# Two unused tiles that move the operands of the one-pass products to multiples of 256 bytes

## The chip, the cores and the metric

The kernel runs on one core of a Trainium2 chip. The metric is the device time of one execution in microseconds. Lower is better.

## The reference, cut to what matters

Two layers, each a linear attention block and an MLP, over 2048 rows of 448 columns in float32:

```python
x = A_x
x = x + _A_ref(_layernorm(x, axis=-1), A_wqkv, A_wo)
x = x + _B_ref(_layernorm(x, axis=-1), B_w1, B_b1, B_w2, B_b2)
x = x + _A_ref(_layernorm(x, axis=-1), A_wqkv, A_wo)
x = x + _B_ref(_layernorm(x, axis=-1), B_w1, B_b1, B_w2, B_b2)
```

`_A_ref` projects x to q, k and v with 16 heads of 28, maps q and k by `phi(t) = where(t > 0, t + 1, exp(t)) + 1e-6`, forms `kv = pk^T v` and `z = sum(pk)` for each head, divides `pq kv` by `pq z + 1e-6` and multiplies by `wo`. `_B_ref` is `gelu(x w1 + b1) w2 + b2` with 1792 hidden columns and the tanh form of gelu.

## The kernel before, in words

**Tiles.** The 2048 rows are 16 tiles of 128, and in the MLP four blocks of four tiles. Every product is float32 in accuracy, but most of them run as one-pass products: both operands are split into a high part of type fp32r and a remainder of type fp32r (`hi`, `lo`), and three products (hi hi, hi lo, lo hi) go into one PSUM bank. A product here is one weight load of the stationary operand (128 columns, PEld in the profile) and one matmul with the moving operand (448 or 512 columns). `pe.matmul(out, stationary, moving, ...)` is the order of the arguments; in the profile's names (`y<-w2h,gh`) the moving operand stands first. Some small products take plain float32 operands and two passes: kvp (L641), mp (L651), zp (L621).

**Stages of a layer.** Phase 1 (`phase1`, L553) walks over the 16 tiles: layer norm, transposes, the projections psk and psq (`proj`, L299, 11 products of 448 columns each) and G (`stage_g`, L475, 11 products). The transition (`ORDER`, L494) turns G into the matrices M for the attention output, and makes the output op of the four tiles of block 0 (`o_mm`, L727, 12 products each). Then comes the MLP: for each block and each of 14 slices i of the hidden columns, `mlp1` (L795) makes hp with 11 products of 512 columns, ACT and DVE make its gelu and split it into gh and gl, and `mlp2` (L814) makes 12 products y of 448 columns, three for each of the block's four tiles. The product of slice i + 1 is issued ahead of y of slice i. Into the steps of a block `behind` (L876) puts the attention output of the next block by a plan written out by hand, in which op comes from `oc_mm` (L736) with 11 products, four times a block.

The order of all instructions is fixed by the program (`tc.manual_schedule()`), and each engine runs its own in that order.

**Where operands lie.** On-chip memory is handed out by pool, in the order `consts`, `wts`, `work`, each pool behind the one before. In a pool, tiles lie in the order in which their tag is first asked for, one tile for each buffer of the tag, and each begins at the next multiple of 32 bytes behind the one before. So an unused tile shifts all that is first asked for after it. All offsets are bytes within a partition. Before the change, in the program as built:

| pool | tiles, in order | offset mod 256 |
|---|---|---|
| consts | ones, ident, mhalf, tiny, zc, mask, b1s, b2b | ones and ident 128 |
| consts | none, za and zb, dc | none 224, za 0 |
| wts | w1h, w1l, w1x, w2h, w2l | 64 |
| work | H (x), S (staging, squares, Mh and half of Ml) | 64 |
| work | bst, bmv, bve, brs (three buffers each, each in 32 bytes) | from 64 on |
| work | tail, W and V pieces (wk, wq, pq), XH, XL, A (xnh, gh), B (xnl, gl), e, E (kh, qh), F (kl, ql, half of Ml), xn | 192 |
| work | dn, rd | 192 and 64 |

Within a tile, the pieces that products read begin at multiples of 512 bytes (128 columns) or 1792 bytes (448 columns), which are multiples of 256, so an operand has the offset mod 256 of its tile. The moving operand of hp is four runs of 128 columns, 2048 bytes apart (`moving`, L224); all other moving operands are one run.

Of the kernel before, what the change touches and what calls it, by code (L numbers as in the profile page):

```python
# [9 lines left out]
F32 = mybir.dt.float32  # L10
# [12 lines left out]
def linear_attn_mlp_kernel(  # L23
# [26 lines left out]
    consts = ctx.enter_context(tc.tile_pool(name="consts", bufs=1))  # L50
    wts = ctx.enter_context(tc.tile_pool(name="wts", bufs=1))
    work = ctx.enter_context(tc.tile_pool(name="work", bufs=2))
# [121 lines left out]
                       compare_op=OP.is_ge, fill=0.0)  # L174
    b1s = consts.tile([128, NF], F32, name="b1s")
    b2b = consts.tile([128, D], F32, name="b2b")

    w1h = wts.tile([128, 3, F], F32R, name="w1h")
    w1l = wts.tile([128, 3, F], F32R, name="w1l")
# [11 lines left out]
    def ln_bn(xs):  # L191
        st = work.tile([128, 6], F32, name="bst", tag="bst", bufs=3)
        dve.bn_stats(st, xs)
        return st

    def ln_stats(xs, st=None):
        st = ln_bn(xs) if st is None else st
        mv = work.tile([128, 2], F32, name="bmv", tag="bmv", bufs=3)
        dve.bn_aggr(mv, st)
        ve = work.tile([128, 1], F32, name="bve", tag="bve", bufs=3)  # L200
        dve.tensor_scalar(ve, mv[:, 1:2], 1e-5, None, op0=OP.add)  # L201
        rs = work.tile([128, 1], F32, name="brs", tag="brs", bufs=3)
        pool.tensor_tensor(rs, ve, mhalf, op=OP.pow)  # L203
        return xs, mv, rs
# [172 lines left out]
    def stage_a(l, t):  # L377
        sts[l, t] = ln_stats(xt.pop((l, t)))

    def stage_n(l, t):  # L380

        xs, mv, rs = sts.pop((l, t))
        dve.tensor_scalar(xs, xs, mv[:, 0:1], rs, op0=OP.subtract, op1=OP.mult)
        xns[l, t] = xs
        if t < TURNED[l]:
            d = tails[l, t] = work.tile([128, 128], F32, name="tail", tag="tail", bufs=2)
            act.copy(d.rearrange("p (u n) -> p u n", u=2), xs[:, None, TL:].to_broadcast([128, 2, 64]))
# [521 lines left out]


    stage_a(0, 0)
    bn = ln_bn(xt[0, 1])
    stage_n(0, 0)
    split_hi("k", 0, st_k)
# [4 lines left out]
    for l in range(LAYERS):  # L919
# [27 lines left out]
        for tok in ORDER.split():  # L947
            name, j = tok.rstrip("0123456789"), int("0" + tok.lstrip("abcdefghijklmnopqrstuvwxyzQTG"))
# [69 lines left out]
```

## Time and profile before

| what | value |
|---|---|
| time, median of 3 runs | 885.9 us (885.64 to 886.61) |
| the profiled execution | 884.81 us |
| its span, first to last instruction | 883.1 us |
| PE busy | 877.8 us, 4182 matmuls |
| DVE, ACT, POOL busy | 489.9, 343.5, 220.8 us |

The page of the profile lists busy times by engine, the chain of work that ended last, and groups of instructions by line. The timeline lists single instructions with their start and duration in us. In the answer by windows each row is a stretch of time, its length, and for each engine its busy time with the number of instructions in it, then the granted clock of PE, the DMA share and GB/s. PE's durations overlap: a matmul's start and the next one's start are nearer to one another than its duration is long.

### The profile page before, as it was taken

The page shows a single profiled execution, that of the slowest core. Times are in us where ns is not written, and L with a number is a line of the kernel's source. Part 1 is how long each engine was busy: PE and PEld are TensorE (multiplying, and loading weights), DVE is VectorE, ACT ScalarE, POOL GpSimd, SP SyncE. Part 2 cuts the span into 40 slices and gives each one's busy share as a digit, 9 for nine tenths or more (in the row PEclk, how much of TensorE's full clock was granted, in tenths as well). Part 3 has the DMA queues.
Part 4 walks back from the last instruction along what each step waited for, and adds up shares of the span by engine and source line. Part 5 has one row for each costly group of instructions (what it writes and reads, how often), then busy time and mean ns, then how long its engine had stood idle before and what let it go on. Part 6 is the DMA issues. An engine that isn't in the chain of part 4 may idle for free.

```text
span 883.1 us, 11676 instructions
## 1 busy us (share of the span) xinstructions
PE 877.8 (99%) x4182; PEld 773.0 (88%) x4182; DVE 489.9 (55%) x953; ACT 343.5 (39%) x603; POOL 220.8 (25%) x250
## 2 busy tenths in 40 slices
PE   9999999999999999999999999999999999999998
PEld 8999888888888888888899998988888888888887
DVE  6878585658455443226477876864664373433112
ACT  5676635334323322333356565332232233233221
POOL 5566532335013102012222344210320140130000
PEclk9999999999999999999999999999999999999999
DMA  5475637633313402051146543352332423111001
GB/s 157 135 231 165 199 88 211 180 99 118 131 59 104 154 0 96 1 178 48 48 133 192 164 127 105 113 171 79 116 106 84 136 72 108 49 48 42 1 1 42
DMA packets 63482, 94.76 MB, mean 107 GB/s; under 512 B 8896, under 2 KB 58560, under 8 KB 63424
## 3 DMA queue, kind: packets, MB, share of 16 engines
q1 hardware_dynamic: 63424, 94.01, 34.0%
q8 instruction: 33, 0.54, 0.3%
q14 instruction: 25, 0.20, 0.1%
HBM read 56.17 MB, written 34.60 MB: 103 GB/s over the span
## 4 chain that ended last, share of the span: by engine, by line
PE 96%; DMA 1%; DVE 1%; ACT 1%; issue 0%; SPq 0%; POOL 0%; DVEq 0%; ACTq 0%; POOLq 0%
PE y L820 10%; PE y L821 10%; PE y L819 10%; PE hp L801 9%; PE hp L803 9%; PE hp L802 9%; PE hp L805 3%; PE hp L804 3%; PE psq L308 2%; PE psq L307 2%; PE psq L306 2%; PE psk L307 2%; PE G L482 2%; PE G L483 2%; PE psk L308 2%; PE G L481 2%
## 5 line engine op out<-in xcount | busy, mean ns | idle before, releaser
L811 DVE TENSOR_TENSOR gl<-g,gh 128x512 fp32r<-128x512 f32 x112 | 83.1, 742 | 306.3 <-ACT gh L810 306.3
L807 ACT ACTIVATE g<-hp,b1s 128x512 f32<-128x512 f32 x112 | 77.2, 689 | 412.5 <-PE hp L805 409.2
L820 PE MATMUL y<-w2l,gh 128*128 128x448 f32 x448 | 164.6, 367 | 0.0
L821 PE MATMUL y<-w2h,gl 128*128 128x448 f32 x448 | 164.0, 366 | 0.0
L819 PE MATMUL y<-w2h,gh 128*128 128x448 f32 x448 | 162.9, 364 | 0.0
L801 PE MATMUL hp<-XH,w1h 128*128 128x512 f32 x336 | 132.8, 395 | 0.0
L803 PE MATMUL hp<-XL,w1h 128*128 128x512 f32 x336 | 132.4, 394 | 0.0
L802 PE MATMUL hp<-XH,w1l 128*128 128x512 f32 x336 | 132.1, 393 | 0.0
L203 POOL TENSOR_TENSOR brs<-bve,mhalf 128x1 f32<-128x1 f32 x64 | 39.5, 617 | 286.5 <-DVE bve L201 283.4
L820 PEld LDWEIGHTS y<-w2l,gh 128*128 128x128 f32 x448 | 84.1, 188 | 10.1
L819 PEld LDWEIGHTS y<-w2h,gh 128*128 128x128 f32 x448 | 84.1, 188 | 9.8
L821 PEld LDWEIGHTS y<-w2h,gl 128*128 128x128 f32 x448 | 84.2, 188 | 6.1
L803 PEld LDWEIGHTS hp<-XL,w1h 128*128 128x128 f32 x336 | 63.1, 188 | 15.1 <-issue 0.5
L802 PEld LDWEIGHTS hp<-XH,w1l 128*128 128x128 f32 x336 | 63.6, 189 | 11.7
L801 PEld LDWEIGHTS hp<-XH,w1h 128*128 128x128 f32 x336 | 63.0, 188 | 11.8
L810 ACT CAST gh<-g 128x512 fp32r<-128x512 f32 x112 | 69.6, 622 | 3.6
L694 POOL TENSOR_TENSOR pz<-pq,zb 128x448 f32<-128x448 f32 x32 | 36.8, 1154 | 87.2 <-DVE dn L700 76.1
L416 POOL TENSOR_TENSOR xnl<-x,xnh 128x384 fp32r<-128x384 f32 x32 | 35.1, 1095 | 71.7 <-ACT xnh L415 39.6
L296 DVE TENSOR_TENSOR XL<-sp,XH 128x512 fp32r<-128x512 f32 x50 | 44.4, 894 | 4.2 <-ACT XH L295 4.2
L805 PE MATMUL hp<-XL,w1x 128*128 128x512 f32 x112 | 44.4, 397 | 0.0
L804 PE MATMUL hp<-XH,w1x 128*128 128x512 f32 x112 | 44.0, 393 | 0.0
L763 POOL TENSOR_TENSOR x<-x,b2b 128x448 f32<-128x448 f32 x32 | 42.0, 1332 | 0.0
(146 smaller groups left out, 1565.0 us busy)
## 6 DMA issues: line engine op xcount, KB each, us to landing
x<-in_A_x_dram SPq DMA_DIRECT2D x32, 224.0 KB, 3.8
pq_d<-eq SPq DMA_DIRECT2D x32, 224.0 KB, 2.9
pq<-pq_d SPq DMA_DIRECT2D x32, 224.0 KB, 3.2
sq_m<-sq SPq DMA_DIRECT2D x14, 512.0 KB, 2.8
sp<-sq_m SPq DMA_DIRECT2D x56, 128.0 KB, 3.0
x<-x_d SPq DMA_DIRECT2D x32, 224.0 KB, 3.4
sq_a<-sq SPq DMA_DIRECT2D x12, 512.0 KB, 2.9
sp<-sq_a SPq DMA_DIRECT2D x48, 128.0 KB, 3.1
```

Source lines behind the costliest of these rows:

```text
L296: eng.tensor_tensor(lo.rearrange("p (c i n) -> p c i n", c=4, n=32), x, f(h), op=OP.subtract)
L801: pe.matmul(o, w1h[:, c, s], x.moving(x.hi, c), start=(c == 0), stop=False)
L802: pe.matmul(o, w1l[:, c, s], x.moving(x.hi, c), start=False, stop=False)
L803: pe.matmul(o, w1h[:, c, s], x.moving(x.lo, c), start=False, stop=False)
L804: pe.matmul(o, w1x[:, s], x.moving(x.hi, 3), start=False, stop=False)
L805: pe.matmul(o, w1x[:, s], x.moving(x.lo, 3), start=False, stop=True)
L807: act.activation(g, hp, AF.Gelu_apprx_tanh, bias=b1s[:, i:i + 1])
L810: act.copy(gh, g)
L811: dve.tensor_sub(gl, g, f(gh))
L819: pe.matmul(acc[j], gh[:, s], w2h[:, i], start=first, stop=False)
L820: pe.matmul(acc[j], gh[:, s], w2l[:, i], start=False, stop=False)
L821: pe.matmul(acc[j], gl[:, s], w2h[:, i], start=False, stop=last)
```

## The change

One tile of 192 bytes is asked for in `consts` behind b2b, one of 128 bytes in `work` behind the small tiles of the first layer norm. Nothing reads or writes either. Of the tiles in the table, ones, ident and those up to b2b stay where they are; all others move.

```diff
     b1s = consts.tile([128, NF], F32, name="b1s")
     b2b = consts.tile([128, D], F32, name="b2b")
+    consts.tile([128, 48], F32, name="space")
 
     w1h = wts.tile([128, 3, F], F32R, name="w1h")
...
     stage_a(0, 0)
+    work.tile([128, 32], F32, name="space", tag="space", bufs=1)
     bn = ln_bn(xt[0, 1])
     stage_n(0, 0)
```

## The prediction

> **What bounds the kernel now.** I read the page first (span, busy shares, granted clock, the chain that ended last), then the groups by line, then the timeline of the tensor engine, stage by stage.
>
> ```profile
> span 883.1 us, 11676 instructions
> PE 877.8 (99%) x4182; PEld 773.0 (88%) x4182; DVE 489.9 (55%) x953; ACT 343.5 (39%) x603; POOL 220.8 (25%) x250
> PEclk9999999999999999999999999999999999999999
> PE 96%; DMA 1%; DVE 1%; ACT 1%; issue 0%; SPq 0%; POOL 0%; DVEq 0%; ACTq 0%; POOLq 0%
> ```
>
> The chain of work that ended last lies on PE for 96% of the span, and the clock was granted in full throughout. So whatever the change does, it does by the rate of PE's products. The engines behind them wait for PE:
>
> ```profile
> L811 DVE TENSOR_TENSOR gl<-g,gh 128x512 fp32r<-128x512 f32 x112 | 83.1, 742 | 306.3 <-ACT gh L810 306.3
> L807 ACT ACTIVATE g<-hp,b1s 128x512 f32<-128x512 f32 x112 | 77.2, 689 | 412.5 <-PE hp L805 409.2
> L820 PE MATMUL y<-w2l,gh 128*128 128x448 f32 x448 | 164.6, 367 | 0.0
> L821 PE MATMUL y<-w2h,gl 128*128 128x448 f32 x448 | 164.0, 366 | 0.0
> L819 PE MATMUL y<-w2h,gh 128*128 128x448 f32 x448 | 162.9, 364 | 0.0
> L801 PE MATMUL hp<-XH,w1h 128*128 128x512 f32 x336 | 132.8, 395 | 0.0
> L803 PE MATMUL hp<-XL,w1h 128*128 128x512 f32 x336 | 132.4, 394 | 0.0
> L802 PE MATMUL hp<-XH,w1l 128*128 128x512 f32 x336 | 132.1, 393 | 0.0
> L805 PE MATMUL hp<-XL,w1x 128*128 128x512 f32 x112 | 44.4, 397 | 0.0
> L804 PE MATMUL hp<-XH,w1x 128*128 128x512 f32 x112 | 44.0, 393 | 0.0
> ```
>
> ACT waits 409.2 us for hp, DVE 306.3 us behind ACT. There are 3 x 448 = 1344 y products and 3 x 336 + 2 x 112 = 1232 hp products. The mean durations here (364 to 397 ns) overlap and are no rates. The rate is the pitch, the distance from one start to the next, and that needs the timeline and counts by window. A window's PEld count is the number of weight loads that began in it, one for each product:
>
> ```profile
> 65.51:81.11 15.60, 15.60 (x79) 14.46 (x77) 14.19 (x29) 10.23 (x20) 8.94 (x12) 1.00 0.58 184
> 277.08:282.08 5.00, 5.00 (x25) 4.32 (x23) 4.20 (x9) 1.83 (x3) 2.65 (x3) 1.00 0.00 0
> 874.22:878.91 4.69, 4.69 (x25) 4.32 (x23) 2.06 (x4) 1.31 (x2) 0.00 (x0) 1.00 0.00 0
> ```
>
> - Attention stage (psk, psq and G): 15.60 us / 77 = 202.6 ns a product of 448 columns.
> - The last y products, which follow one another without hp: 4.69 / 23 = 203.9 ns, also 448 columns.
> - One step of the MLP (12 y, 11 hp): 5.00 us. With y at 203.9 ns, hp takes (5000 - 2447) / 11 = 232.1 ns.
>
> G (L481 to L485) and y (L819 to L821) have the same shape and the same rhythm, three products to a PSUM bank, and their stationary operands even lie in the same buffers (xnh and gh in A, xnl and gl in B). Only the moving operand differs: kh and kl begin 192 bytes past a multiple of 256, w2h and w2l 64 bytes past one. Higher address bits don't matter: from one i to the next, w2 moves on by 1792 bytes and A and B change buffers, and the step stays at 5.00 us. Nor does the stage itself matter: where 11 op products (moving wq at 192, stationary qh and ql at 192) join an MLP step, these two starts lie 12 + 11 + 11 = 34 products apart:
>
> ```profile
> 171.50 0.36 PE L819 MATMUL y<-w2h,gh 128*128 128x448 f32 x1
> ...
> 178.73 0.36 PE L819 MATMUL y<-w2h,gh 128*128 128x448 f32 x1
> ```
>
> That is 7.23 us, 2.23 more than the 23, so 202.7 ns for each op: the attention rate, in the MLP stage. I read from it that a product pays for how the low address bits of its moving operand stand to those of the stationary operand that is loaded beside it. An equal offset mod 256 (192 and 192) gives 202.6 ns, and a distance of 128 (y: 64 and 192) gives 203.9.
>
> **The change part by part.** Neither tile is ever used, so no instruction, wait or DMA is added, taken away or reordered; every queue issues what it did. Only addresses move. In the program as built before, the weights w1 and w2 and the tiles H and S begin at 64 mod 256, and the small tiles follow; the work tiles W, V, XH, XL, A, B, e, E, F and xn begin at 192 mod 256. The first space adds 192 bytes ahead of the weights: 64 + 192 = 256. The second adds 128 behind the four kinds of small tile: 192 + 192 + 128 = 512. So every one-pass operand comes to 0 mod 256, and hp (moving 192, stationary 64) and y (moving 64, stationary 192) go from a distance of 128 to a distance of 0.
>
> - **y**: 1344 x (203.9 - 202.6) = 1.7 us less.
> - **hp**: no row shows a 512-column product at distance 0. From one side, it gains what y gains, 1.3 ns. From the other, its whole surplus falls to that of the attention products. For the surplus I need a floor, and take it from the two-pass products:
>
> ```profile
> 109.25 3.31 PE L641 MATMUL kvp<-gt,stg 128*112 128x112 f32 x32
> 115.50 3.17 PE L651 MATMUL mp<-wot,kvm 112*112 112x448 f32 x8
> L641 PE MATMUL kvp<-gt,stg 128*112 128x112 f32 x64 | 6.6, 262 | 0.0
> L651 PE MATMUL mp<-wot,kvm 112*112 112x448 f32 x16 | 6.3, 539 | 0.0
> ```
>
> Less the last one's own duration, 32 kvp start at (3310 - 262) / 31 = 98.3 ns and 8 mp at (3170 - 539) / 7 = 375.9 ns: 0.826 ns a column and 5.8 ns fixed. Half of that a column, and the same fixed part, would make a one-pass product of 448 columns 190.8 ns and one of 512 columns 217.3 (an estimate). The surplus over this floor is then 11.8 ns in attention, 13.1 for y and 14.8 for hp, and hp would gain 3.0 ns. hp could also gain nothing, if its surplus comes from reading four runs of 128 columns. Between 1.3 and 3.0 I take 2.0, nearer the y row: 1232 x 2.0 = 2.5 us less.
> - **op of block 0 (L732 to L734)**: Mh and two of four Ml lie at 64 in S, against A and B at 192: 80 of 96 products, 1.3 ns each, 0.1 us less.
> - **psk, psq, G, op by chunks**: 32 x 33 + 24 x 11 = 1320 products. Distance 0 before and after, so nothing, unless the offset itself matters; that is unknown. At most they gain their 11.8 ns, 15.6 us.
> - **The other engines**: their operands move too. Were each of their instructions a little slower or faster, the waits above (409.2 and 306.3 us) hide it. It costs only where PE waits for them, and the chain gives DVE and ACT 1% each.
> - **DMA**: same sizes and order, 1% of the chain; nothing.
>
> Sum: 1.7 + 2.5 + 0.1 = 4.3 us. The profiled execution took 884.8 us (span 883.1 and 1.7 around it), 1.1 under the median of 885.9. The sum is a difference, so I take it off the median: 881.6 us. With hp at nothing or at 3.0 ns, this case's own range is 880 to 884.1. PE stays the bound: a step of 4.96 us still holds only 4.20 us of DVE and 1.83 of ACT.
>
> **A rule against it.** The row: 203.9 and 202.6 ns at one shape, 13.1 and 11.8 over the floor. The Trainium skill ("TensorE: Matmul & The Clock Gate", Step-by-step: what each phase is for) says that PE reads moving and stationary operands through two independent ports, so that loading the next weights takes no read bandwidth from the running matmul. By that rule no distance between the two could matter, and the sum would be 0 instead of 4.3 us; the rows for y and G disagree, though they can't say whether the port or something behind it is shared.
>
> **Rivals.**
>
> *Nothing changes (885.9 us).* The difference between G and y has another cause than offsets, such as the steps of w2 itself. For it: 1.3 ns is 0.6% of a pitch. Against it: equal shapes, equal rhythm, equal stationary buffers, and op at 202.7 in the same stage. The Trainium skill ("SBUF — State Buffer", Specifications (TRN2)) gives lines of 16 bytes; by that line size every operand is aligned already and 256 brings nothing. No row here shows a line's size.
>
> *The alignment itself pays (about 874 us).* A 448-column row of 1792 bytes that begins at 64 or 192 touches 8 pieces of 256 bytes, an aligned one 7; a weight load of 512 bytes touches 3, then 2. For hp, the four runs of 512 bytes touch 12, then 8. If the surplus over the floor goes with the pieces, it falls from 11 to 9 for 448 columns and from 15 to 10 for 512: 13.1 x 0.18 x 1344 = 3.2 us, 11.8 x 0.18 x 1416 = 3.0 us, 14.8 x 0.33 x 1232 = 6.0 us, together 12 us. For it: the one-pass products alone carry the surplus. Against it: no product here begins at 0. All the surplus gone would be 18 + 18 + 17 = 53 us, an outer bound.
>
> *PE settles into a slower rhythm (893 us).* In psq after the products of block 0, these starts lie six apart:
>
> ```profile
> 137.45 0.37 PE L306 MATMUL psq<-wq,XH 128*128 128x448 f32 x1
> ...
> 138.69 0.37 PE L310 MATMUL psq<-wq,XH 128*128 128x448 f32 x1
> ```
>
> 1.24 / 6 = 206.7 ns, where the same operands at the same offsets took 202.6 before. So one set of addresses has two steady rhythms, 4.1 ns apart, and which one a stretch falls into hangs on how it began. If, with the new offsets, the MLP steps fall into the slow one, y loses 206.7 - 203.9 = 2.8 ns and hp, I assume, as much: 2.8 x (1344 + 1232) = 7.2 us more. It decides as soon as an MLP step takes more than 5.00 us. For it: the rhythm exists at distance 0. Against it: nearly all of phase 1 ran in the quick one, and a step that mixes 512 and 448 columns starts its rhythm anew each time.
>
> **How the numbers follow.** Forecast 42%; the alignment itself pays 25%; nothing 10%; slower rhythm 23%. A measurement can tell about 0.2% (1.8 us) from no change, so faster 0.67, same 0.10, slower 0.23. The range takes in the slow rhythm and most of the alignment case, which could be half as much again as reckoned: 866 to 893.5. It leaves out the outer bound and a slow rhythm that takes in phase 1 too.
>
> **What the changed profile would show.** The instruction count stays at 11676 and the order the same. An MLP step falls from 5.00 to about 4.96 us, a lone y from 203.9 to 202.6 ns, and attention stays at 202.6. If attention falls too, the alignment itself pays; if the step rises towards 5.06, the slower rhythm has taken over; if the step stays at 5.00, offsets were not the cause. A forecast built on one distance is wrong if offset 0 behaves unlike 64 and 192, which no row of before can exclude.

## The result and the profile after

The changed kernel takes 878.5 us (median of 6 runs, 878.22 to 879.46) against 885.4 us (median of 6 runs, 884.24 to 886.61): a ratio of 0.9925, interval 0.9912 to 0.9938. That is 6.9 us or 0.75% less; 4.3 us was forecast.

The page of the profile after, the lines that answer to those shown of before:

```profile
span 876.9 us, 11676 instructions
PE 870.9 (99%) x4182; PEld 771.9 (88%) x4182; DVE 489.9 (56%) x953; ACT 343.5 (39%) x603; POOL 220.9 (25%) x250
PEclk9999999999999999999999999999999999999999
PE 97%; DMA 1%; DVE 0%; POOL 0%; SPq 0%; issue 0%; ACT 0%; POOLq 0%; DVEq 0%
L812 DVE TENSOR_TENSOR gl<-g,gh 128x512 fp32r<-128x512 f32 x112 | 83.1, 742 | 300.7 <-ACT gh L811 300.7
L808 ACT ACTIVATE g<-hp,b1s 128x512 f32<-128x512 f32 x112 | 77.2, 689 | 406.2 <-PE hp L806 402.7
```

The instruction count is the same, and so are the busy times of DVE, ACT and POOL to 0.1 us. DVE and ACT wait some 6 us less for PE. The chain still lies on PE. All lines behind the first space count one higher in this file.

Where did the 6.2 us of span go? Each row is a layer's MLP from its first y to the end of its last one, first of before, then of after:

```profile
144.28:445.87 301.59, 301.59 (x1399) 262.73 (x1398) 152.97 (x287) 97.31 (x159) 63.35 (x59) 1.00 0.30 96
577.51:878.91 301.40, 301.40 (x1399) 262.54 (x1397) 129.74 (x250) 84.77 (x134) 41.71 (x39) 1.00 0.22 71
```

```profile
144.38:442.88 298.50, 298.50 (x1399) 262.53 (x1398) 152.59 (x287) 97.33 (x159) 63.29 (x59) 1.00 0.30 97
574.45:872.75 298.30, 298.30 (x1399) 262.34 (x1397) 129.98 (x250) 84.78 (x134) 41.65 (x39) 1.00 0.22 72
```

3.09 and 3.10 us, so all of it went in the two MLPs. Smaller pieces, of after: one MLP step, the last y products, and 435 attention products of layer 2. The PEld count is the number of products:

```profile
270.98:275.92 4.94, 4.94 (x24) 4.32 (x23) 3.26 (x6) 1.83 (x3) 1.46 (x2) 1.00 0.17 54
868.09:872.75 4.66, 4.66 (x25) 4.32 (x23) 2.05 (x4) 1.31 (x2) 0.00 (x0) 1.00 0.00 0
443.90:532.06 88.16, 88.16 (x437) 81.71 (x435) 66.70 (x135) 50.58 (x93) 28.17 (x41) 1.00 0.50 160
```

The attention stretch of before, for comparison:

```profile
446.90:535.06 88.16, 88.16 (x437) 81.69 (x435) 66.68 (x134) 50.53 (x93) 28.12 (x41) 1.00 0.52 159
```

The step falls from 5.00 to 4.94 us. A lone y falls from 203.9 to 4.66 / 23 = 202.6 ns, which leaves (4940 - 12 x 202.6) / 11 = 228.1 ns for hp, 4.0 less than before. The attention stretch is unchanged to 0.01 us: 88.16 / 435 = 202.7 ns. The timeline of a step after shows how hp gets there:

```profile
273.41 0.39 PE L802 MATMUL hp<-XH,w1h 128*128 128x512 f32 x1
273.64 0.40 PE L803 MATMUL hp<-XH,w1l 128*128 128x512 f32 x1
273.88 0.39 PE L804 MATMUL hp<-XL,w1h 128*128 128x512 f32 x1
274.11 0.39 PE L802 MATMUL hp<-XH,w1h 128*128 128x512 f32 x1
...
275.92 0.36 PE L820 MATMUL y<-w2h,gh 128*128 128x448 f32 x1
```

By the starts to the nanosecond, on the mean of the 84 steps without op, the first three hp take 231.4 ns each (before: 230.6) and the other eight 226.8 (before: 232.5). So hp begins each step near its old pitch and then settles into a quicker rhythm.

### The profile page after: what moved, and what is told of

Its sections match the earlier page's. It is cut to its first block, busy times and chain, and to the rows that moved or that the text cites. A ratio compares the mean times of both kernels' runs of the same rounds, so it can differ in the third digit from the quotient of the medians.

```text
span 876.9 us, 11676 instructions
## 1 busy us (share of the span) xinstructions
PE 870.9 (99%) x4182; PEld 771.9 (88%) x4182; DVE 489.9 (56%) x953; ACT 343.5 (39%) x603; POOL 220.9 (25%) x250
## 4 chain that ended last, share of the span: by engine, by line
PE 97%; DMA 1%; DVE 0%; POOL 0%; SPq 0%; issue 0%; ACT 0%; POOLq 0%; DVEq 0%
PE y L822 10%; PE y L820 10%; PE y L821 10%; PE hp L803 9%; PE hp L804 9%; PE hp L802 9%; PE hp L806 3%; PE hp L805 3%; PE psq L307 2%; PE psk L308 2%; PE psq L309 2%; PE psq L308 2%; PE psk L309 2%; PE G L483 2%; PE psk L307 2%; PE G L482 2%
```

## The experiments

Three theories stood against each other: that the distance mod 256 between moving and stationary operand counts, that the multiple of 256 itself counts, and that a stretch keeps the rhythm in which it began, whatever the addresses. All kernels are the one before with unused tiles at other places; nothing is computed differently (e12 adds one product whose result nothing reads). "0 apart" means that both operands have the same offset mod 256. Ratios are against the kernel before.

| kernel | hp moving past stationary | y moving past stationary | step, us | last y, ns | attention of layer 2, ns | ratio (interval) |
|---|---|---|---|---|---|---|
| before | 128 | 128 | 5.00 | 204.0 | 202.7 | 1 |
| changed | 0 | 0 | 4.94 | 202.7 | 202.7 | 0.9925 (0.9912 to 0.9938) |
| e1, all at 64 | 0 | 0 | 4.94 | 202.7 | 202.7 | 0.9931 (0.9916 to 0.9946) |
| e5, all at 32 | 0 | 0 | 4.94 | 202.7 | 202.7 | 0.9925 (0.9912 to 0.9939) |
| e2, first space alone | 128 | 128 | 5.00 | 204.0 | 202.7 | 0.9999 (0.9989 to 1.0008) |
| e3, hp alone | 0 | 128 | 4.94 | 203.6 | 202.7 | 0.9934 (0.9917 to 0.9950) |
| e4, y alone | 128 | 0 | 5.05 | 206.7 | 206.7 | 1.0092 (1.0077 to 1.0107) |
| e6 | +32 | -32 | 5.01 | 204.6 | 206.7 | 1.0034 (1.0023 to 1.0045) |
| e7 | +64 | -64 | 4.97 | 202.3 | 206.7 | 0.9983 (0.9974 to 0.9992) |
| e8 | +96 | -96 | 5.04 | 206.4 | 206.7 | 1.0080 (1.0065 to 1.0095) |
| e10 | 0 | -64 | 4.96 | 202.1 | 206.7 | 0.9964 (0.9951 to 0.9978) |
| e11 | 0 | +64 | 4.93 | 200.3 | 202.7 | 0.9910 (0.9896 to 0.9924) |

The step, the last y (23 products) and the attention column (435 products, always 0 apart) are read in each profile as above. The table's last y is from starts to the nanosecond; the two decimals of the windows below give it to within 0.3 ns.

### e1: the second space alone, everything at 64

```diff
     stage_a(0, 0)
+    work.tile([128, 32], F32, name="space", tag="space", bufs=1)
     bn = ln_bn(xt[0, 1])
```

> The second space alone, of 128 bytes: every operand of a one-pass product lies at 64 mod 256, none at a multiple of 256, and moving and stationary operand are 0 apart in hp, in y and in the attention stage. If the distance between the two is what counts, it is as fast as the changed kernel: hp 228.0 ns, y 202.7 ns, an MLP step of 4.94 us, about 878.5 us. If the multiple of 256 itself counts, it stays at 5.00 us a step and about 885.4 us. If each stretch of products falls into its rhythm by how it begins, hp and y may come out at yet other values, such as 206.7 ns for y.

Measured: 878.9 us, a step of 4.94 us. A step of this kernel by windows:

```profile
276.98:281.92 4.94, 4.94 (x25) 4.32 (x24) 4.20 (x9) 1.83 (x3) 2.64 (x3) 1.00 0.02 3
```

No operand of a one-pass product lies at a multiple of 256, and the whole gain is there. So the multiple of 256 isn't what counts; the distance is.

### e2: the first space alone

```diff
     b2b = consts.tile([128, D], F32, name="b2b")
+    consts.tile([128, 48], F32, name="space")
```

> The first space alone, of 192 bytes: the weights, H and S lie at multiples of 256, XH, XL, A, B, E, F, W and V at 128 mod 256. hp and y stay 128 apart. By the distance: as before, 5.00 us a step, hp 232.1, y 203.9, about 885.4 us. By the multiple of 256: y has its moving operand aligned and hp its stationary one, so each gains something, about 880 to 883 us.

Measured: 884.9 us against 885.1 for the kernel before. A step:

```profile
276.65:281.65 5.00, 5.00 (x25) 4.32 (x23) 4.20 (x9) 1.83 (x3) 2.66 (x3) 1.00 0.00 0
```

The weights at a multiple of 256 alone bring nothing. Of the change's two tiles, the second does all, because it alone alters the distance.

### e5: everything at 32

```diff
+    consts.tile([128, 56], F32, name="space")
...
+    work.tile([128, 32], F32, name="space", tag="space", bufs=1)
```

> Spaces of 224 and 128 bytes: every operand of a one-pass product at 32 mod 256, moving and stationary 0 apart everywhere. If only the distance counts: as the changed kernel, an MLP step of 4.94 us, hp 228, y 202.7, 878.5 to 879 us. If operands must begin at a multiple of 64 bytes at least: slower, by one more piece per operand, hp and y both up by several ns, attention too, 885 us or more.

Measured: 878.3 us, a step of 4.94 us (the table's row). Operands that begin at 32 mod 256 are as quick as those at 0 or 64.

### e3 and e4: hp alone, y alone

Both shift w2 by 128 bytes against w1; e4 shifts the work tiles with it, so that y comes together instead of hp.

```diff
     w1x = wts.tile([128, F], F32R, name="w1x")
+    wts.tile([128, 32], F32, name="mid")
```

For e4 also:

```diff
     stage_a(0, 0)
+    work.tile([128, 32], F32, name="space", tag="space", bufs=1)
```

> One space of 128 bytes between w1x and w2h: w1 at 64, w2 at 192, the work tiles at 64. hp is 0 apart, y stays 128 apart, nothing is a multiple of 256. By the distance: hp 228.0, y 203.9, a step of 11 x 228.0 + 12 x 203.9 = 4.955 us, 108 steps x 0.045 = about 4.9 us faster than before, 880.5 us. By the multiple of 256: no change, 885.4 us. By a rhythm that hp and y share: the gain is split otherwise, hp between 228 and 232.

> 128 bytes between w1x and w2h and 128 behind the small tiles: w1 at 64, w2 and the work tiles at 192. y is 0 apart, hp stays 128 apart. By the distance: y 202.7, hp 232.1, a step of 4.985 us, about 1.7 us faster than before, 883.7 us. By the multiple of 256: no change. By a rhythm that hp and y share: y not at 202.7.

Measured: hp alone 879.1 us, 0.66% less. y alone 893.4 us, 0.92% more. The profile of hp alone, a step and the last y, then the first hp of a step and the y behind its eleven hp:

```profile
276.65:281.59 4.94, 4.94 (x24) 4.32 (x23) 4.20 (x9) 1.83 (x3) 2.64 (x3) 1.00 0.01 3
868.87:873.55 4.68, 4.68 (x24) 4.32 (x23) 2.05 (x4) 1.31 (x2) 0.00 (x0) 1.00 0.00 0
```

```profile
851.56 0.39 PE L802 MATMUL hp<-XH,w1h 128*128 128x512 f32 x1
...
854.05 0.37 PE L820 MATMUL y<-w2h,gh 128*128 128x448 f32 x1
```

hp alone is even better for hp than both together: from the first on, without the slow start, it takes 226.8 ns by the starts to the nanosecond (mean of 84 steps). y stays at 4.68 / 23 = 203.5, yet the step is the same 4.94 us: what y loses, hp gets back. The profile of y alone, a step, the last y, and the 435 attention products:

```profile
867.26:872.31 5.05, 5.05 (x25) 4.33 (x23) 0.69 (x1) 1.31 (x2) 0.00 (x0) 1.00 0.00 0
882.40:887.16 4.76, 4.76 (x25) 4.32 (x23) 2.08 (x4) 1.31 (x2) 0.00 (x0) 1.00 0.00 0
450.08:539.98 89.90, 89.90 (x436) 81.68 (x435) 66.69 (x134) 50.61 (x93) 27.97 (x41) 1.00 0.51 156
```

y is 0 apart and should run at 202.6 ns; it runs at 4.76 / 23 = 206.9. The attention products behind the MLP, 0 apart before and after, run at 89.90 / 435 = 206.7 instead of 202.7 and keep it for all 435. So distance is not all: at distance 0 there are two steady rhythms for 448 columns. The parts don't add up: hp alone -0.66%, y alone +0.92%, both -0.75%.

Is the slow rhythm there because hp is 128 apart? The trace of y alone speaks against so simple a rule. Its first MLP step, and 187 attention products (17 groups of 11) of layer 1:

```profile
144.82:149.80 4.98, 4.98 (x25) 4.33 (x23) 1.40 (x4) 1.31 (x2) 0.17 (x1) 1.00 0.74 253
54.07:92.72 38.65, 38.65 (x189) 35.11 (x187) 30.10 (x59) 25.85 (x50) 22.81 (x29) 1.00 0.63 198
```

The first four steps of layer 1, with hp 128 apart as ever, took 4.98 us each, as the distance had it (4.985): y at 202.4 ns, hp at 231.9. The change came in the next three steps, which op had joined (op at 202.4, 203.0, then 205.9 ns); the steps behind them stayed at 5.05, those of layer 2 too. And attention ran at 38.65 / 187 = 206.7 ns before the kernel's first hp; from 97.81 us on, behind a pause, 33 such products with the same offsets took 202.6 each. So neither hp's distance nor the addresses alone set the rhythm; what came before does, and the trace doesn't show by what rule. The quick steps don't prove a gain of y by itself either: the kernel before, with y 128 apart, has one step of 4.98 us in each layer, the third.

### e6, e7, e8: 32, 64 and 96 apart

The second space alone, with 160, 192 and 224 bytes:

```diff
     stage_a(0, 0)
+    work.tile([128, 40], F32, name="space", tag="space", bufs=1)
```

> The second space with 160 bytes: weights, H and S at 64, work tiles at 96 mod 256. hp has its moving operand 32 bytes past its stationary one, y 32 short of it; the attention stage stays 0 apart. If the distance acts by whether the two streams meet in the same piece of memory, 32 should lie near one of the two values known, hp 226.7 to 228 or 232 and y 202.7 or 204; if the cost grows evenly from 0 to 128 apart, a quarter of the way: hp 229, y 203, about 880 us. If only how a stretch begins decides, y at 206.7 is possible as in the kernel that moved y alone (893 us).

> The second space with 192 bytes: weights, H and S at 64, work tiles at 128 mod 256. hp is 64 apart, y 64 the other way. If the cost grows evenly: halfway, hp 230, y 203.3, about 882 us. If pieces of 64 bytes in four kinds decide, a value of its own, maybe the best of all: hp 226.7 (two pieces of 16 columns over the bare 512) and y 200.0 (two over 448), a step of 4.89 us, about 873 us.

> The second space with 224 bytes: weights, H and S at 64, work tiles at 160 mod 256. hp is 96 apart, y 96 the other way. If the cost grows evenly: three quarters of the way, hp 231, y 203.6, about 884 us. If pieces decide, as at 64 or as at 128 apart (885 us).

Measured: 887.8, 883.3 and 892.1 us. The cost doesn't grow evenly from 0 to 128: a step takes 5.01, 4.97 and 5.04 us, against 4.94 at 0 and 5.00 at 128. In all three the attention stretch of layer 2 took the slow rhythm (89.90 us for 435 products), 1.7 us more in each, though its operands are 0 apart. The table's last y, read in layer 2, stood at 204.6, 202.3 and 206.4 ns, so attention and y need not share a pitch. 64 apart was the best of the three, but not the best of all that I held possible.

### e9: the operand beside it, or its own?

```diff
+    wts.tile([128, 32], F32, name="mid")
     w2l = wts.tile([128, NF, D], F32R, name="w2l")
...
         h = t512("A", 2, "xnh", F32R)
+        if (l, t) == (0, 0):
+            work.tile([128, 32], F32, name="space1", tag="space1", bufs=1)
         lo = t512("B", 2, "xnl", F32R)
+        if (l, t) == (0, 0):
+            work.tile([128, 32], F32, name="space2", tag="space2", bufs=1)
```

> Spaces that put w2l and B (gl, xnl) 128 bytes past w2h and A (gh, xnh), with w1, XH, XL at 64. In y the products go (gh, w2h), (gh, w2l), (gl, w2h). Each moving operand then is 0 apart from the stationary operand that is loaded beside it for the next product, but 0, 128 and 128 apart from its own. If the operand loaded beside it counts: y 202.7 with the even pattern of the changed kernel (or the steady 206.7), a step of 4.94 us, about 879 us. If its own stationary operand counts: y near 204 with starts that jump between 196 and 212 ns as before the change.

Measured: 879.2 us, a step of 4.95 us, the last y at 203.1 ns (from the starts to the nanosecond); attention 88.36 us for 435. That is neither the 202.7 of the one reading nor, with starts between 199 and 207 ns apart, the jumps between 196 and 212 of the other. Within the steps y takes 202.8 ns on the mean, near the first reading, but in the same other pattern. It doesn't settle which stationary operand the distance is to be taken to.

### e10 and e11: hp at 0, y at 64 to either side

```diff
     w1x = wts.tile([128, F], F32R, name="w1x")
+    wts.tile([128, 16], F32, name="mid")
...
     stage_a(0, 0)
+    work.tile([128, 16], F32, name="space", tag="space", bufs=1)
```

This is e11; e10 has 48 columns in place of 16, twice.

> Try for a better kernel: 192 bytes between w1x and w2h, 192 behind the small tiles. hp and attention are 0 apart, w2 lies 64 bytes short of A and B. With hp and y 64 apart, y alone ran at 202.3 ns in the last stretch, the lowest so far. If each group had its own pitch by its distance: hp 226.6 to 228, y 202.3, a step of 4.92 to 4.94 us, 876.5 to 879 us. If the start of a stretch decides the rhythm: y in a slow one at 206 or hp at 231, 883 us or more.

> The same with w2 64 bytes past A and B: 64 bytes between w1x and w2h, 64 behind the small tiles. If only the size of the distance mod 256 counts and not its sign: as with w2 64 short. If the order of the two streams counts, another value; nothing run so far shows +64 for y. hp at +64 took about 230.6 ns where 228 was seen at 0 and 232 at 128, so I expect y between 202.3 and 204, a step of 4.93 to 4.96 us, 878 to 881 us.

Measured: 882.0 us with w2 64 bytes short of A and B, 877.1 with w2 64 past them. The sign counts. e10 has the quick y it was made for (202.1), but hp, though 0 apart, takes 230.6 ns, and the attention stage 206.7. e11 beats the changed kernel: 877.1 us (876.36 to 877.26) beside 878.3 (878.13 to 878.53) for e5, which has the changed kernel's distances and ran with it. In the last y products of e11 these two starts lie 21 products apart:

```profile
867.01 0.36 PE L822 MATMUL y<-w2h,gl 128*128 128x448 f32 x1
...
871.21 0.37 PE L822 MATMUL y<-w2h,gl 128*128 128x448 f32 x1
```

4.20 / 21 = 200.0 ns, the quickest pitch of 448 columns in any of these runs.

### e12: y alone, with a break ahead of layer 2's attention

e4, and:

```diff
     for l in range(LAYERS):
         tr = SimpleNamespace(mp={})
+        if l:
+            pe.matmul(bank("m", 2, "brk")[:, :128], ones, ones, start=True, stop=True)
```

> The kernel that moved y alone (w1 at 64, w2 and the work tiles at 192; its attention stretch of layer 2 ran 451 products at 206.7 ns), with one two-pass product of 128 columns ahead of layer 2's first attention product, whose result nothing reads. If a stretch keeps the rhythm in which it began, and a break lets it begin anew: the 451 products fall to 202.7 ns in about two cases of three, by the restarts seen so far, 1.8 us less than that kernel's 893.4 for 0.2 to 0.4 us spent; in the third they stay at 206.7. If the rhythm hangs on addresses alone: they stay at 206.7 for certain. Layer 1's share and the MLP steps are unchanged by it.

Measured: 893.3 us, and the 435 products again in 89.90 us. The break did not bring the quick rhythm. That is the outcome which fits both readings (a restart that falls into the slow rhythm again, or no effect), so it tells nothing apart. Against addresses alone there is e4's trace: layer 1's attention, at one set of offsets, ran first at 206.7 and then at 202.6 ns.

## Why the prediction was right, and where it was off

- **What bounds the kernel**: right. Only PE's pitch changed; DVE, ACT and POOL have the same busy time.
- **The distance between the operands**: shown, by e1 and e5 (no multiple of 256, full gain) against e2 (weights at a multiple of 256, no gain).
- **y, 1.7 us**: it measured 1344 x (203.9 - 202.6) = 1.7 us. But no run shows it as a gain that y has by itself: e4 gave y the same distance, and after four quick steps (202.4 ns) y lost 2.5 ns in a step and 2.7 in the last products. The forecast, which summed part by part, had put that into a rival and not into the sum.
- **hp, 2.5 us: the step that was mis-sized.** Forecast 2.0 ns a product within 1.3 and 3.0; measured 4.0, so 1232 x 4.0 = 4.9 us. The upper end assumed that hp's surplus over the two-pass floor could fall no lower than that of the attention products, 11.8 ns. It fell to 228.1 - 217.3 = 10.8 in the changed kernel and to 226.8 - 217.3 = 9.5 in e3: eight of a step's eleven hp run at 226.8 ns, and attention's surplus is no bound for hp. The floor itself was read wrongly. The program has 16 kvp and 4 mp products a layer and the trace 32 and 8 records, so a record is one pass already and half of its time per column has no ground. That the halved slope (0.413 ns a column) is near the 0.42 between the quickest pitches of the two widths (last section) is luck.
- **Attention, no change**: right, 88.16 us for 435 products before and after.
- **Sum**: 1.7 + 4.9 = 6.6 us from the terms, against 6.2 in the spans and 6.9 in the medians. The terms are a little above the spans, in part because the 24 steps with op in them gained less: they fell from 7.23 to 7.18 us.
- **The range**: 878.5 us lies within 866 to 893.5, which was drawn wide for the rivals, but below the forecast's own 880 to 884.1. The direction and the distance as the mechanism were right; the size was too small by hp's term. Part of the gap is the starting point: the forecast went from 885.9 us, and the kernel before took 885.4 in the six runs compared.
- **op of block 0, 0.1 us**: too small to be told; the two MLPs hold 6.19 of the 6.2 us.
- **The rival of alignment itself**: fallen, by e1, e2 and e5.
- **The rival of no change**: fallen. The Trainium skill ("TensorE: Matmul & The Clock Gate", Step-by-step: what each phase is for) says that loading the next weights takes no read bandwidth from the running matmul. What the prediction drew from it, that no distance could matter, doesn't hold here: shifting the work tiles by 128 bytes against the weights made y 1.2 ns and hp 4.0 ns quicker (e1), and hp 5.3 in e3. No run shows through which part of the chip, so the sentence on the ports itself is not tested.
- **The slower rhythm**: it didn't come in the changed kernel, but the mechanism is real: in e4 the steps fell into it and the time came out near the rival's, 893.4 us against 893. That the two agree is partly luck: the rival put 7.2 us on the MLPs and none on attention, while of the 8.2 us in e4's span 5.8 lie in the two MLPs and the rest outside them. The forecast gave it a point of decision (a step over 5.00 us), which e4 crossed with 5.05. That the changed kernel escaped it was not worked out beforehand; the argument that mixed widths start the rhythm anew at each step is refuted by e4, where it held from one step to the next; that phase 1 ran in the quick one was no safety, since in e4 much of phase 1 ran in the slow one.

What stays open: to which stationary operand the distance counts (e9); what picks the rhythm, and what made e4's steps change over from the quick one to the slow one (e4, e12); whether y gains by itself; which hardware the two streams meet in. Not tried: attention's operands at +64 apart, as y in e11.

## What to carry to other kernels

In a kernel bound by one-pass products, read the pitch from the starts in the timeline, not the durations, and compare stretches of the same shape: 1.3 ns there led to 0.75% here. What counted was the offset of the moving operand against the stationary one, mod 256, and not a round address: one unused tile of 128 bytes did as much as the pair, and 64 apart for one group did better. Don't add up the groups' gains: the same offsets ran at two pitches, which depend on what came before in a way not worked out here; measure the combination.

## What the runs showed of the hardware beyond that

Long stretches settle at fixed pitches, among them 200.0 ns (e11's y), 202.7, 204.0 and 206.7 for 448 columns, and 226.8 for 512 (e3's hp). The quickest of each width differ by 26.8 ns for 64 columns, 0.42 ns a column, so the slow rhythm of 206.7 lies about 16 columns (6.7 ns) above the quickest (an estimate). The Trainium skill ("TensorE: Matmul & The Clock Gate", Back-to-back issue gap) gives N / 2.4 + 2.5 ns for an isolated gap, which would be 189 and 216 ns (estimates from that page); no one-pass stretch here came nearer than 200.0 and 226.8.
